# The feed-forward layer's last casts and products written ahead of the first expert's steps; rank and table transposes written later

## The chip, the cores and the metric

One core of a Trainium2 chip runs the kernel. The metric is the device time in microseconds (us) of one execution; the time before is the median of three runs. Matrix products run on TensorE (PE, with its weight loads as PEld), elementwise work on VectorE (DVE), ScalarE (ACT) and GpSimd (POOL); SyncE (SP) issues most transfers.

## What is computed

Three layers in float32: a gated linear attention (4 sequences of 768 tokens, 8 heads of 48), a feed-forward layer with softplus (384 to 2048 to 384), and a layer of 8 experts of which each token takes at most one.

```python
# attention: state = f * state + k (x) v ; y = q . state          -> x [3072, 384]
h = x @ w_in
g = np.maximum(h, 0.0) + np.log1p(np.exp(-np.abs(h)))
x = g @ w_out
# experts
do_compute = x @ w_skip > 0
logits = xc @ w_gate                      # xc = x[do_compute]
e_idx = np.argmax(logits, axis=1)
gate_w = softmax(logits)[e_idx]
y[mask] = gate_w[mask, None] * (np.maximum(xc[mask] @ w1[e], 0.0) @ w2[e])   # per expert e
out[do_compute] = xc + y                  # the other tokens keep x
```

## The kernel before

The 3072 tokens are worked in 12 units of 256. Every float32 operand of a large product is split into a high part (fp32r) and a low part, and three products of the parts stand for one. The attention runs in 24 chunks of 128 tokens and is worked in between the feed-forward layer's steps.

**The feed-forward layer.** A unit has 8 steps (`STEPS`), one for every 256 hidden columns. `Ffn.up` (L396) makes 18 products into a PSUM tile `ph`; `ph` and the experts' `phm` share two PSUM buffers (tag "h"). `act_a` (L411 to L416) computes exp(-|h|) and max(h, 0) into tiles `u` and `w`, `act_b` (L422, L423) the logarithm on ACT and the sum on POOL (on DVE for the very last step of the last unit, which is also worked in two halves, `FINE`), `act_c` (L431, L432) casts the result to `gh` and `gl`. `down` (L443) adds 12 products into `acc0` and `acc1`, one per 128 tokens. `u`, `w`, `gh` and `gl` have two buffers each. The loop over s (L853) writes step s's `up`, the step before's `act_b` and `act_c`, and the `down` of the step before that; the program text numbers the last unit's steps 0 to 7, and s = `total` - 1 is step 7. What the loop leaves over, `act_b` and `act_c` of step 7 and `down` of steps 6 and 7, is written in the part after it.

**Routing.** After a unit's last `down`, `evac` copies `acc` out on ACT, `logits` and `choose` find each token's expert on DVE, `rank` (L502, L503 on PE, then DVE) gives each token its place in that expert's list, and `scatter` (L511, POOL) writes token numbers into a table in DRAM. `table_cols` (L538) loads that table back with eight transfers on SP into a tile `rows`, which takes one of the two `u` buffers, turns it with two PE transposes (`pids`, L547) and copies it to `tab`. Unit 11's tokens do not go through the table: `last_rank` ranks them and builds one-hot tiles (`place`, L518 to L527), and `last_ids` multiplies these on PE (`placed`, L533, `pplace`) and adds `tab`; the sum is the list of token numbers that the remaining gathers need. `flag_counts` sets the flag for the general path.

**The experts.** The fullest expert is worked first, its first 256 tokens (`firsts`) from a list that is ready earlier. `turn` (L694, `pxg`, then L373 and L374) transposes the gathered rows; four steps follow, each with `Tiles.up` (L711, 18 products into `phm`), `act` (L720, L721) and, one step later, `down` (L756, 24 products into `pom`, which takes the PSUM buffers of `acc0` and `acc1`). The loop over `at` (L1018) writes these steps, with `later` as the list of `down`s still to come. `turn` of `firsts` stands at s = `total` - 3.

**Order.** The program text is not the final order. A scheduler places each engine's instructions by the order of writing and its own picture of when inputs are ready; where `pin` is on (it is switched on in `last_down`), an instruction keeps its place in the text. The engines run their rows strictly in order.

Of the kernel before, what the change touches and what calls it, by code (L numbers as in the profile page):

```python
# [37 lines left out]
def gla_softplus_moe_kernel(  # L38
# [17 lines left out]
    NCH, PR, _ = q.shape  # L56
# [14 lines left out]
    STEPS = NF // 2  # L71
# [480 lines left out]
    def set_turns():  # L552

        pc = psm("pfirst")
        te.matmul(pc[:, 0:E], lhsT=ones, rhs=cnt_acc[:, 0, :], start=True, stop=True)
        tmp = lambda nm, n: ffn.tile([P, n], F32, tag="t" + nm, name="t" + nm, bufs=1)
        c, mx, at, neg = tmp("c", E), tmp("m", 1), tmp("a", E), tmp("n", E)
        ve.tensor_tensor(c, pc[:, 0:E], ebase, op=ALU.subtract)
        ve.tensor_reduce(mx, c, axis=AX.X, op=ALU.max)
        ve.scalar_tensor_tensor(c, c, mx, down8, op0=ALU.is_ge, op1=ALU.mult)  # L560
        ve.tensor_reduce(mx, c, axis=AX.X, op=ALU.max)

        ve.tensor_scalar(at, down8, mx, -1.0, op0=ALU.subtract, op1=ALU.mult)
        ve.tensor_scalar(neg, at, 0.0, float(E), op0=ALU.is_lt, op1=ALU.mult)
        ve.tensor_tensor(at, at, neg, op=ALU.add)
        ve.tensor_scalar(erot, at, float(NT), float(-BIG), op0=ALU.mult, op1=ALU.add)
        ve.tensor_scalar(c, down8, -1.0, float(E), op0=ALU.mult, op1=ALU.add)
        ve.tensor_tensor(perm, at.unsqueeze(1).to_broadcast([P, E, E]), c.unsqueeze(2).to_broadcast([P, E, E]),
                         op=ALU.is_equal)
        ve.tensor_scalar(c, c, mx, float(E), op0=ALU.subtract, op1=ALU.add)  # L570
        ve.tensor_scalar(neg, c, float(E), float(-E), op0=ALU.is_ge, op1=ALU.mult)
        ve.tensor_tensor(turns, c, neg, op=ALU.add)
        expert_at.extend(nc.values_load(turns[0:1, e:e + 1], engines=[sy.engine], min_val=0, max_val=E - 1)
                         for e in range(E))
# [51 lines left out]
    def w_load(n):  # L626
        e, g = n // 4, n % 4
        raw[n] = w_tile(n, F32)
        src = (w1 if g < 2 else w2)[ds(expert_at[e], 1), g % 2].rearrange("o p c -> (o p) c")
        sy.dma_start(out=raw[n].rearrange("p a c -> p (a c)"), in_=src)  # L630
# [16 lines left out]
    def feed(n):  # L647

        while True:
            while wanted and len(slots) >= (1 if wanted[0][0] == "load" else 2):  # L650
                what, q = wanted.pop(0)
                if what == "load":
                    w_load(q)
                else:
                    pieces.extend(w_split(q))
            if n <= 0 or not pieces:
                return
            w_piece(*pieces.pop(0))
            n -= 1
# [140 lines left out]
    if True:  # L800
# [22 lines left out]
        def attention_step(s):  # L823
            for c, nm in sorted(todo.pop(s, []), key=lambda x: (x[0], order[x[1]])):
                ops[nm](c)
# [5 lines left out]
        def route_step(u, i):  # L831
            if u < 0 or u >= NU:
                return
            if i == 1:
                routes[u] = Route(ffns[u], u * UNIT, tid[:, u * CPU:(u + 1) * CPU], *([pools["pre"], cnt_last] if u == NU - 1 else []))
            for at, nm, *a in ROUTE if u < NU - 3 else ROUTE_SOON if u < NU - 1 else ():
                if at == i:
                    getattr(routes[u], nm)(*(a if nm != "rank" else [cnt_acc[:, 0, :]]))
            if i == 2 and 0 < u < NU - 2:
                routes[u - 1].scatter(1)  # L840
# [3 lines left out]
        def conv(s, j):  # L844
            if s in CONV_AT:
                g = CONV_AT.index(s)
                if j % 2:
                    conv_w(g, j // 2)
                if j == 3 and g + 2 < STEPS:
                    load_w(g + 2)  # L850
        total = NU * STEPS
        last_att = 4 * NCH - 2 - STEPS
        for s in range(-20, total):  # L853
            u, i = divmod(s, STEPS)
            conv(s, 0)
            if s > 0:
                pu, pi = divmod(s - 1, STEPS)
                ffns[pu].act_b(pi)
            conv(s, 1)
            if s >= 0:  # L860
                if i == 0:
                    ffns[u] = Ffn(xhl[u], FINE if u == NU - 1 else ())
                ffns[u].up(i)
            if s > 0:
                ffns[pu].act_c(pi)
            if s >= 0:
                ffns[u].act_a(i)
            conv(s, 2)
            attention_step(s + STEPS + 1)
            conv(s, 3)  # L870
            if s >= 2:
                pu, pi = divmod(s - 2, STEPS)
                ffns[pu].down(pi)
            route_step(u - 1, i)
            if s == total - 2 * STEPS:
                set_turns()
                for n in range(4):
                    w_load(n)
            if s == last_att:
                first.close()  # L880
                pools["pre"] = rest.enter_context(tc.tile_pool(name="pre", bufs=1, side="right", reuse_waits="tile"))
                slots += [("pre", f"w{i}") for i in range(5)]
                wanted += [("split", n) for n in range(4)] + [("load", n) for n in range(4, 12)] + [("split", n) for n in range(4, 8)]
                for e in range(2, E):
                    wanted += [("split", n) for n in range(4 * e, 4 * e + 4)]
                    if e + 1 < E:
                        wanted += [("load", n) for n in range(4 * e + 4, 4 * e + 8)]
            if u == NU - 1:
                slots.append(("wp", f"s{i}"))
                if pu == u and pi % 2:  # L890
                    slots.extend(("wp", f"s{STEPS + pi - 1 + n}") for n in range(2))
            if s > last_att:
                feed(PIECES if s <= last_att + 4 else 1)
            if s == last_att + 2:
                first_ids()
                firsts = Tiles(0, [id0[:, 0, t:t + 1] for t in range(2)], ("acc0", "acc1"))
                firsts.fetch([id0[:, 1, t:t + 1] for t in range(2)], NT - 2 * UNIT)
            if s == total - 4:
                table_cols()
                last_base()  # L900
            if s == total - 3:
                firsts.turn()
                flags()
# [91 lines left out]
    ffn_end = ffns[NU - 1]  # L995
# [10 lines left out]
    def last_rank():  # L1006
        last.rank(cnt_all)
        last.place()

    def last_ids():  # L1010
        set_ids(last.placed())
        flag_counts()

    later = [[(ffn_end.down, STEPS - 2)], [(last_down,)]]
    seq = [(w, i) for w in work for i in range(len(w.steps))]
    fetched, turned = 1, 1
    ffn_end.act_b(STEPS - 1)
    for at in range(len(seq) + 2):  # L1018
        if at < len(seq):
            w, i = seq[at]  # L1020
            while pieces and pieces[0][0] <= 4 * w.e + (1 if i == 0 else 3):
                w_piece(*pieces.pop(0))
            now, then = w.steps[i]
            for f, *args in now:
                f(*args)
            if at == 0:
                ffn_end.act_c(STEPS - 1)
            turn_at = 0 if w.n == 1 else 3 if w is firsts else 2
        for _ in range(2 if len(later) > 1 and (at == 2 or (at > 2 and w.n == 2 and i)) else 1):
            for f, *args in later.pop(0) if later else ():  # L1030
                f(*args)
        if at < len(seq):
            later += then
        feed(FILL[at])
        if at == 1:
            last_rank()
        elif at == 2:
            last_ids()
        if at >= 2 and at < len(seq):
            k0 = work.index(seq[at][0])  # L1040
            while fetched < len(work) and fetched <= k0 + 1:
                work[fetched].fetch(work[fetched].cols)
                fetched += 1
            if turned == k0 + 1 and turned < fetched and i == turn_at:
                work[turned].turn()
                turned += 1
# [9 lines left out]
    with tc.If(some > 0, preferred_fallthrough_block=False), ExitStack() as gen:  # L1056
# [23 lines left out]
        for e in range(E):  # L1080
            n = nc.values_load(cnt[0:1, e:e + 1], min_val=0, max_val=NT)
            with tc.If(n > 0):
# [6 lines left out]
                with tc.For_i(0, (n + (P - 1)) // P, 1) as it:  # L1089
# [3 lines left out]
                    w = Tiles(e, [c[:, 1:2]], ("acc0",))  # L1093
# [75 lines left out]
```

## Time and profile before

| | us |
|---|---|
| median of 3 runs | 752.81 (750.46 to 754.51) |
| the profiled execution | 751.03 |
| its span in the trace | 749.3 |
| outside the span | 1.73 |
| PE busy | 688.8 (92%) |
| DVE busy | 538.5 (72%) |
| ACT busy | 477.2 (64%) |
| POOL busy | 199.3 (27%) |

The sums of the prediction are made against the profiled execution, and the difference is then put on the median. PE is busy nearly all the time, so a look at the whole tells little; what counts is where PE stands still. A timeline row gives start, duration, engine, line, tiles and, in brackets, the idle time before it and what ended it. A matmul's end is modelled and lies about one matmul behind the start of the next, so from one start to the next is the better measure of lost time.

### The profile page before, as it was taken

Reading aid. Unit: us, or ns where it says so; the run is one execution under the profiler, and the core shown is the slowest. Engines: PE = TensorE matmul, PEld = TensorE weight load, DVE = VectorE, ACT = ScalarE, POOL = GpSimd, SP = SyncE. Lnnn points to the kernel's source line nnn. Section 1 sums busy time; section 2 is a strip of 40 time slices with the busy share of each in tenths; the row PEclk is TensorE's granted clock in tenths of the full one; section 3 lists DMA queues with packets and bytes.
Section 4 is the critical chain, followed back from the end, with each engine's and each line's share of the span. In section 5 each row is a group of like instructions: output and inputs, shape, how many; then the busy total and the mean of one; then the engine's idle time right before and its main releaser. Section 6 shows DMA issues by size and latency. Waiting matters only on the chain. (4 is left out here: it accounts for less than half of the span.)

```text
span 749.3 us, 15063 instructions
## 1 busy us (share of the span) xinstructions
PE 688.8 (92%) x5869; PEld 639.8 (85%) x5869; DVE 538.5 (72%) x1081; ACT 477.2 (64%) x864; POOL 199.3 (27%) x170
## 2 busy tenths in 40 slices
PE   1788889999999999999999999999979979999993
PEld 1576768989999999999999999999969878989893
DVE  6989999867777677778767777756667555866851
ACT  5596777767666766766686666656567634555750
POOL 1204212322222323222232322223333204222111
PEclk9989999999999999999999999999999999999997
DMA  9944423202132121212212121100606412555910
GB/s 278 282 159 147 151 66 111 80 26 74 55 82 73 50 64 52 87 56 76 77 41 70 45 85 44 61 9 1 210 22 219 166 43 82 189 210 198 324 43 11
DMA packets 33905, 77.19 MB, mean 103 GB/s; under 512 B 5967, under 2 KB 18594, under 8 KB 33824
## 3 DMA queue, kind: packets, MB, share of 16 engines
q1 hardware_dynamic: 31456, 71.89, 29.7%
q0 software_dynamic: 2368, 4.25, 2.0%
q8 instruction: 48, 0.79, 0.5%
q14 instruction: 33, 0.27, 0.1%
HBM read 64.89 MB, written 12.11 MB: 103 GB/s over the span
## 5 line engine op out<-in xcount | busy, mean ns | idle before, releaser
L396 PE MATMUL ph<-xh,wi 128*128 128x256 f32 x1152 | 229.1, 288 | 3.2 <-ACT wi L215 1.6
L423 POOL TENSOR_TENSOR w<-w,u 128x512 f32<-128x512 f32 x95 | 129.3, 1361 | 354.0 <-DVE u L416 204.5
L396 PEld LDWEIGHTS ph<-xh,wi 128*128 128x128 f32 x1152 | 187.2, 192 | 8.2 <-ACT wi L215 2.3
L396 PE MATMUL ph<-xl,wi 128*128 128x256 f32 x576 | 163.9, 285 | 0.0
L443 PE MATMUL acc<-wo_hi,gh 128*128 128x394 f32 x384 | 137.8, 360 | 2.2 <-ACT gh L431 2.2
L443 PE MATMUL acc<-wo_hi,gl 128*128 128x394 f32 x384 | 130.1, 346 | 3.8 <-DVE gl L432 3.6
L443 PE MATMUL acc<-wo_lo,gh 128*128 128x394 f32 x384 | 131.7, 343 | 0.0
L396 PEld LDWEIGHTS ph<-xl,wi 128*128 128x128 f32 x576 | 110.8, 192 | 0.0
L432 DVE TENSOR_TENSOR gl<-w,gh 128x512 fp32r<-128x512 f32 (+1 forms) x97 | 67.0, 692 | 43.1 <-ACT gh L431 42.5
L415 DVE SCALAR_TENSOR_TENSOR u<-w,u 128x512 f32<-128x512 f32 (+1 forms) x97 | 66.7, 689 | 34.3 <-ACT w L413 33.9
L411 ACT ACTIVATE u<-ph 128x512 f32<-128x512 f32 (+1 forms) x97 | 56.9, 587 | 46.5 <-PE ph L396 44.9
L422 ACT ACTIVATE w<-w 128x512 f32<-128x512 f32 (+1 forms) x97 | 60.9, 628 | 37.0 <-DVE u L415 36.9
L443 PEld LDWEIGHTS acc<-wo_hi,gh 128*128 128x128 f32 x384 | 72.4, 189 | 7.9 <-ACT gh L431 3.3
L431 ACT CAST gh<-w 128x512 fp32r<-128x512 f32 (+1 forms) x97 | 59.2, 611 | 30.4 <-POOL w L423 26.2
L443 PEld LDWEIGHTS acc<-wo_hi,gl 128*128 128x128 f32 x384 | 72.6, 189 | 5.4 <-DVE gl L432 5.1
L443 PEld LDWEIGHTS acc<-wo_lo,gh 128*128 128x128 f32 x384 | 73.1, 190 | 0.2 <-DVE wo_lo L243 0.2
L416 DVE SCALAR_TENSOR_TENSOR u<-ph,u 128x512 f32<-128x512 f32 (+1 forms) x97 | 65.9, 680 | 3.3
L641 DVE TENSOR_TENSOR w<-w,w 128x768 fp32r<-128x768 f32 x64 | 59.5, 973 | 7.5 <-ACT w L640 4.7
L412 ACT ACTIVATE u<-u 128x512 f32<-128x512 f32 (+1 forms) x97 | 60.7, 627 | 1.6
L413 ACT ACTIVATE w<-u 128x512 f32<-128x512 f32 (+1 forms) x97 | 60.5, 625 | 1.4
L756 PE MATMUL pom<-w,gh 128*128 128x384 f32 x208 | 54.2, 342 | 2.5 <-DVE om L766 2.5
L640 ACT CAST w<-w 128x768 fp32r<-128x768 f32 x64 | 49.8, 837 | 3.1 <-DMA w<-in_moe_w_dram 2.3
(194 smaller groups left out, 1134.6 us busy)
## 6 DMA issues: line engine op xcount, KB each, us to landing
w<-in_moe_w_dram SPq DMA_DIRECT2D x32, 768.0 KB
si<-in_moe_w_in_dram SPq DMA_DIRECT2D x8, 768.0 KB
so<-in_moe_w_out_dram SPq DMA_DIRECT2D x8, 768.0 KB
f<-in_f_logit_dram SPq DMA_DIRECT2D x24, 227.5 KB
q<-in_q_dram SPq DMA_DIRECT2D x24, 224.0 KB
k<-in_k_dram SPq DMA_DIRECT2D x24, 224.0 KB
x_s<-xr SPq DMA_DIRECT2D x24, 192.5 KB
v<-in_v_dram SPq DMA_DIRECT2D x24, 192.0 KB
```

The source lines that it names most:

```text
L396: te.matmul(ph[:, j, :], lhsT=w[i][:, kk, j * P:(j + 1) * P], rhs=x[:, kk, :], start=(n == 0), stop=(n == 3 * KD - 1))
L411: se.activation(u[:, c], ph[:, c], AF.Abs)
L412: se.activation(u[:, c], u[:, c], AF.Exp, scale=-1.0)
L413: se.activation(w[:, c], u[:, c], AF.Identity, bias=1.0)
L415: ve.scalar_tensor_tensor(u[:, c], w[:, c], 1.0, u[:, c], op0=ALU.subtract, op1=ALU.subtract)
L416: ve.scalar_tensor_tensor(u[:, c], ph[:, c], 0.0, u[:, c], op0=ALU.max, op1=ALU.subtract)
L422: se.activation(w[:, c], w[:, c], AF.Ln)
L423: (ve if i in self.fine else ge).tensor_tensor(w[:, c], w[:, c], u[:, c], op=ALU.add)
L431: se.copy(flat(gh)[:, c], w[:, c])
L432: ve.tensor_tensor(flat(gl)[:, c], w[:, c], flat(gh)[:, c].bitcast(F32), op=ALU.subtract)
L443: te.matmul(self.acc[t][:, 0:XR], lhsT=g[:, j, t * P:(t + 1) * P], rhs=w[f // 4][:, f % 4, :], start=(f == 0 and n == 0), stop=(f == NF - ...
L641: pin(ve.tensor_tensor(lo, t, hi.bitcast(F32), op=ALU.subtract))
```

## The change

`table_cols` and `last_base` move from s = `total` - 4 to s = `total` - 2, that is, behind the last `turn` and the flags. `down` of step 6 and `act_c` of step 7 move ahead of the experts' loop; `later` starts with an empty entry instead. `last_rank` moves from the end of round `at` = 1 into round `at` = 2, behind the first `down` of the experts that this round writes. Nothing is added or removed: each engine has as many instructions as before.

```diff
-            if s == total - 4:
+            if s == total - 2:
                 table_cols()
                 last_base()
             if s == total - 3:
...
-    later = [[(ffn_end.down, STEPS - 2)], [(last_down,)]]
+    later = [[], [(last_down,)]]
     seq = [(w, i) for w in work for i in range(len(w.steps))]
     fetched, turned = 1, 1
     ffn_end.act_b(STEPS - 1)
+    ffn_end.down(STEPS - 2)
+    ffn_end.act_c(STEPS - 1)
     for at in range(len(seq) + 2):
...
-            if at == 0:
-                ffn_end.act_c(STEPS - 1)
             turn_at = 0 if w.n == 1 else 3 if w is firsts else 2
-        for _ in range(2 if len(later) > 1 and (at == 2 or (at > 2 and w.n == 2 and i)) else 1):
+        for n in range(2 if len(later) > 1 and (at == 2 or (at > 2 and w.n == 2 and i)) else 1):
             for f, *args in later.pop(0) if later else ():
                 f(*args)
+            if at == 2 and n == 0:
+                last_rank()
         if at < len(seq):
             later += then
         feed(FILL[at])
-        if at == 1:
-            last_rank()
-        elif at == 2:
+        if at == 2:
             last_ids()
```

Two places show what this does to the engines' rows. The first is the end of the feed-forward layer on PE. Before, from the last product of step 4's `down` (`acc1`, `gl_7417`) to the first of the experts' `phm0`; `ph7` is step 7's `up`, `wo_hi2_119` with `gh_7486` step 5's `down`:

```order
L443 MATMUL acc1_7230<-wo_hi2_119,gl_7417 128x394
L547 MATMUL pids_7387<-ident_79,rows_7378 128x96
L694 MATMUL pxg_7445<-ident_79,xg_7124 128x128 x3
L694 MATMUL pxg_7451<-ident_79,xg_7128 128x128 x3
L784 MATMUL pm_7459<-ident_79,hm_7457 1x128
L785 MATMUL pm_7459<-ident_79,col0_98 1x128
L396 MATMUL ph7_7515<-xh11_6650,wi7_114 128x256
...
L547 MATMUL pids_7387<-ident_79,rows_7378 128x96
L443 MATMUL acc0_7229<-wo_hi2_119,gh_7486 128x394
...
L711 MATMUL phm0_7573<-xh_7443,w0_7061 128x256
```

The same place in the changed kernel (`gh_7469` is step 5's `down`, `gh_7534` and `gl_7535` step 6's):

```order
L443 MATMUL acc1_7230<-wo_hi2_119,gl_7400 128x394
L396 MATMUL ph7_7515<-xh11_6650,wi7_114 128x256
...
L711 MATMUL phm0_7591<-xh_7426,w0_7061 128x256
...
L443 MATMUL acc0_7229<-wo_hi2_119,gh_7469 128x394
...
L443 MATMUL acc0_7229<-wo_hi3_121,gh_7534 128x394
...
L547 MATMUL pids_7505<-ident_79,rows_7496 128x96
L443 MATMUL acc0_7229<-wo_hi3_121,gl_7535 128x394
```

The two table transposes now stand around the second part of step 6's `down`; `pxg` and `pm` are gone from here, since they now stand 102 products earlier, beside unit 10's rank; and `phm0` follows step 7's `up` directly. The same stretch on POOL, before, from step 2's sum (`w_7223`); `table` is the scatter of unit 10's two halves, and the last two sums are those of steps 5 and 6:

```order
L423 TENSOR_TENSOR w_7223<-w_7223,u_7222 128x512
L511 DMA table_76<-tid_87,rslot_7264 24576x1
L423 TENSOR_TENSOR w_7302<-w_7302,u_7301 128x512
L511 DMA table_76<-tid_87,rslot_7264 24576x1
L423 TENSOR_TENSOR w_7358<-w_7358,u_7357 128x512
L423 TENSOR_TENSOR w_7421<-w_7421,u_7420 128x512
L423 TENSOR_TENSOR w_7491<-w_7491,u_7490 128x512
```

And in the changed kernel:

```order
L423 TENSOR_TENSOR w_7223<-w_7223,u_7222 128x512
L423 TENSOR_TENSOR w_7302<-w_7302,u_7301 128x512
L511 DMA table_76<-tid_87,rslot_7264 24576x1
L423 TENSOR_TENSOR w_7358<-w_7358,u_7357 128x512
L511 DMA table_76<-tid_87,rslot_7264 24576x1
L423 TENSOR_TENSOR w_7404<-w_7404,u_7403 128x512
L423 TENSOR_TENSOR w_7474<-w_7474,u_7473 128x512
```

Both scatters have moved one sum later, and the second now stands ahead of step 5's sum instead of step 4's. The second place is unit 11's rank on PE, before, from the last product of step 7's `down`:

```order
L443 MATMUL acc1_7230<-wo_hi3_121,gl_7597 128x394
L502 MATMUL pr_7678<-roh_7663,before_83 128x16
L503 MATMUL pr_7678<-cnt_last_94,ones_82 128x16
L711 MATMUL phm2_7703<-xh_7443,w1_7063 128x256
...
L756 MATMUL pom_7727<-w2_7069,gl_7634 128x384
L533 MATMUL pplace_7752<-pcol_7696,prow_7695 128x192
```

And in the changed kernel, where `gl_7611` is the last product of the experts' first `down`:

```order
L443 MATMUL acc1_7230<-wo_hi3_121,gl_7586 128x394
L711 MATMUL phm2_7678<-xh_7426,w1_7063 128x256
...
L756 MATMUL pom_7702<-w2_7069,gl_7611 128x384
L502 MATMUL pr_7715<-roh_7663,before_83 128x16
L503 MATMUL pr_7715<-cnt_last_94,ones_82 128x16
L756 MATMUL pom_7701<-w2_7069,gh_7633 128x384
...
L533 MATMUL pplace_7752<-pcol_7733,prow_7732 128x192
```

The rank has moved behind 18 products of `phm2` and 12 of `pom`; between it and `pplace` stand 12 products now, where 42 stood. On DVE the change in the chain between these two is one row (the difference of the two kernels):

```order
 L506 TENSOR_TENSOR rw<-pr,roh 128x16
+L721 SCALAR_TENSOR_TENSOR gl<-phm_7678,gh 128x512
 L507 TENSOR_REDUCE rrk<-rw 128x2
 L508 TENSOR_SCALAR rslot<-rrk 128x2
...
 L526 TENSOR_SCALAR prow<-place,rcols 128x128
 L527 TENSOR_SCALAR pcol<-place,rcols,rless 128x192
-L721 SCALAR_TENSOR_TENSOR gl<-phm_7703,gh 128x512
```

The low part of `phm2`'s result now stands inside the rank's chain. SP's rows are the same.

## Rows read from the trace of the kernel before

**Rows 1.** The page, busy time and share of the span by engine.

```profile
PE 688.8 (92%) x5869; PEld 639.8 (85%) x5869; DVE 538.5 (72%) x1081; ACT 477.2 (64%) x864; POOL 199.3 (27%) x170
```

**Rows 2.** Windows: length, busy time of PE, PEld, DVE, ACT, POOL, granted clock, DMA.

```profile
592.00:613.00 21.00, 15.53 (x107) 14.28 (x106) 11.89 (x35) 10.50 (x24) 2.55 (x2) 1.00 0.07 23
700.00:720.00 20.00, 20.00 (x112) 17.99 (x111) 16.50 (x22) 15.17 (x24) 2.90 (x2) 1.00 0.62 240
```

**Rows 3.** PE's timeline, 592 to 613 us: the rows around its four stops.

```profile
592.25 0.34 PE L443 MATMUL acc<-wo_hi,gl 128*128 128x394 f32 x1
593.91 0.27 PE L547 MATMUL pids<-ident,rows 96*128 96x96 f32 x1 [1.33 <-DMA rows<-table]
...
599.12 0.34 PE L443 MATMUL acc<-wo_hi,gl 128*128 128x394 f32 x1
600.86 0.36 PE L711 MATMUL phm<-xh,w 128*128 128x256 f32 x1 [1.40 <-DVE u L416]
...
607.19 0.34 PE L443 MATMUL acc<-wo_hi,gl 128*128 128x394 f32 x1
607.84 0.45 PE L443 MATMUL acc<-wo_hi,gh 128*128 128x394 f32 x1 [0.32 <-ACT gh L431]
...
609.74 0.52 PE L443 MATMUL acc<-wo_hi,gl 128*128 128x394 f32 x2
612.68 0.36 PE L502 MATMUL pr<-roh,before 128*128 128x16 f32 x2 [2.42 <-DVE xr L489]
```

**Rows 4.** PE's timeline: first rows of two `phm` groups, of what follows each, and `pplace`.

```profile
603.79 0.28 PE L711 MATMUL phm<-xh,w 128*128 128x256 f32 x1
...
605.92 0.35 PE L443 MATMUL acc<-wo_hi,gl 128*128 128x394 f32 x1
...
613.12 0.41 PE L711 MATMUL phm<-xh,w 128*128 128x256 f32 x1
...
616.86 0.51 PE L756 MATMUL pom<-w,gh 128*128 128x384 f32 x2
...
621.07 0.81 PE L533 MATMUL pplace<-pcol,prow 128*128 128x192 f32 x4
```

**Rows 5.** Windows (columns as above): behind the longest stop, and behind a stop of 1.76 us.

```profile
612.60:617.00 4.40, 4.32 (x23) 4.35 (x24) 2.29 (x14) 0.00 (x0) 0.00 (x0) 0.61 0.34 120
675.00:680.00 5.00, 4.82 (x33) 4.82 (x34) 2.73 (x4) 1.33 (x3) 2.95 (x2) 1.00 0.55 157
```

**Rows 6.** Timelines of ACT and DVE: `act_a` of steps 5, 6 and 7.

```profile
595.82 0.61 ACT L411 ACTIVATE u<-ph 128x512 f32<-128x512 f32 x1
597.32 0.38 ACT L411 ACTIVATE u<-ph 128x256 f32<-128x256 f32 x1 [0.90 <-PE pids L547]
...
592.43 0.69 DVE L416 SCALAR_TENSOR_TENSOR u<-ph,u 128x512 f32<-128x512 f32 x1
...
600.03 1.02 DVE L416 SCALAR_TENSOR_TENSOR u<-ph,u 128x512 f32<-128x512 f32 x2
```

**Rows 7.** Timelines of PE (end of step 5's `up`), POOL (scatters, a sum) and SP (eight loads).

```profile
585.98 0.34 PE L443 MATMUL acc<-wo_hi,gh 128*128 128x394 f32 x1
...
579.42 1.22 POOL L511 DMA_INDIRECT table<-tid,rslot  x1 [0.83 <-DVE rslot L508]
...
586.12 1.02 POOL L511 DMA_INDIRECT table<-tid,rslot  x1 [3.91 <-DMA table<-tid,rslot]
587.14 1.32 POOL L423 TENSOR_TENSOR w<-w,u 128x512 f32<-128x512 f32 x1
...
590.60 3.90 SPq L542 DMA_DIRECT2D rows<-table  x8
```

**Rows 8.** DVE's timeline: first and last row of the rank's chain, and `phm2`'s low part.

```profile
613.31 0.17 DVE L506 TENSOR_TENSOR rw<-pr,roh 128x16 f32<-128x16 f32 x1 [0.37 <-PE pr L503]
...
615.09 0.38 DVE L527 TENSOR_SCALAR pcol<-place,rcols,rless 128x192 f32<-128x192 f32 x1
...
619.62 0.69 DVE L721 SCALAR_TENSOR_TENSOR gl<-phm,gh 128x512 fp32r<-128x512 f32 x1 [4.15 <-ACT gh L720]
```

## Prediction

> **What bounds the kernel now.** I read the page first: PE is busy 92% of the span, the next engine 72% [rows 1]. So what a change is worth is the time in which PE stands still or runs slowly, and only in the stretch that the change touches. The windows show where: between 592 and 613 us PE is busy 15.53 of 21 us, while later stretches such as 700 to 720 us have no idle time at all [rows 2]. PE's timeline then names the four stops of that stretch and what ended each [rows 3]: the table transposes wait for the `rows` load, the experts' first `phm` for DVE to have read step 6's `ph`, step 7's `down` for its cast, and unit 11's rank for the routing chain on DVE.
>
> I measure a stop from start to start, less one product. A product takes 0.18 us: 24 of them run from 616.86 to 621.07 [rows 4]. The stops then cost 593.91 - 592.25 - 0.18 = 1.48, 600.86 - 599.12 - 0.18 = 1.56, 607.84 - 607.19 - 0.18 = 0.47, and 612.68 - (609.74 + 0.18) - 0.18 = 2.58 us [rows 3], together 6.09.
>
> The last stop has a sequel. The 18 products of `phm` take 605.92 - 603.79 = 2.13 us before it and 616.86 - 613.12 = 3.74 us after it [rows 4]; the granted clock of that stretch is 0.61, so part of it ran at 1.2 instead of 2.4 GHz [rows 5]. That is another 1.61 us. In all 7.70 us are lost here.
>
> **The change, part by part.** The instructions stay the same on every engine, so the sum is made of waits alone.
>
> *The table's load and transposes.* The first stop goes, because step 7's `up` no longer stands behind the transposes. The load has a second effect that the stop's row does not show. `rows` holds one of the two `u` buffers from its load, issued at 590.60 [rows 7], until PE has turned it: step 6's first ACT row starts only at 595.82 and step 7's at 597.32, the latter released by `pids` [rows 6]. So DVE reads step 6's `ph` as late as 600.03 [rows 6], and this is what the experts' first `phm` waits for. With `rows` asked for after step 6's tiles, steps 5 and 6 have both buffers, and the second stop should go with the first.
>
> What is late next? I count from the end of step 5's `up` (585.98 before, [rows 7]). PE then has 12 + 18 + 12 products until step 7's `up`, 592.25 + 0.18 - 585.98 = 6.45 us [rows 3, 7]. That `up` needs the PSUM buffer that DVE frees with step 5's L416, which before ended at 592.43 + 0.69 = 593.12, or 7.14 after the same point [rows 6]. In the changed order ACT takes step 5's first row earlier but puts three weight casts into the middle of the chain. So PE waits between 0 and 0.7 us here; I take 0.5, near the row. Step 6's two DVE rows follow, 1.4 us, to 8.5; PE gets to `phm0` at 7.14 + 2.13 = 9.3, so that wait is nil with 0.8 us to spare.
>
> POOL and SP: the load may go once POOL has read step 5's `u`. Its log on ACT and its sum (1.32 us, [rows 7]) should be done by 8.5 + 1.3 = 9.8. The first transpose could start 593.91 - 590.60 = 3.31 us after the first load was issued, [rows 3, 7], so at 13.1; PE gets there at 9.3 + 2.13 + 16 x 0.18 = 14.3. The second needs the last four loads. All eight take 3.90 us to issue; the fourth was issued by 592.55 and had landed 1.36 later, so the eighth is there 3.90 + 1.36 = 5.3 after the first, at 15.1, and PE comes at 14.3 + 0.1 + 8 x 0.18 = 15.8. No wait, with 0.7 to 1.2 us to spare. The load also needs the second scatter. The scatters stand one sum later on POOL, behind a rank result that now has four DVE rows of up to 0.69 us [rows 6] more ahead of it; that makes some 3 us, so 582.5 in the clock of before. The second started 6.70 us after the first, since it waits for the first one's landing, and landed 3.46 us after its end [rows 7]; by the same steps it now lands at 582.5 + 6.7 + 1.0 + 3.5 = 593.7, against 585.98 + 9.8 = 595.8 for the sum. What stands behind the second scatter on POOL is step 5's sum instead of step 4's, and that one is not ready before it either. So I cost the scatters at nothing; the cover is 2 us.
>
> The transposes of the gathered rows and the flag move forward into a stretch where PE is full. They cost the same there as they did here, so this is nothing, from both sides.
>
> *Step 6's `down` and step 7's cast and products.* Between the two halves of step 7's `down` now stand the 18 products of `phm1`, 2.13 us, so the second half's cast has time. I let the third stop go, 0.47 us, with 0 as the other end.
>
> *The rank.* The fourth stop was 2.58 us of waiting for the copy of `acc` and the choice. Now `phm2` (2.13) and 12 products (2.1) stand ahead of the rank, 4.2 us, so the wait is covered. `pom` takes over `acc0` and `acc1`, so its first product needs the copy; that copy was the first part of the same 2.58 us, and `phm2` alone covers 2.13 of them. At most 0.5 us, taken as nothing. With the stop the slow clock should go too: behind a stop of 1.76 us at 675 us the clock stayed at 1.00, behind this one it fell to 0.61 [rows 3, 5], and no stop that I now expect is over 0.7 us.
>
> The price is a new wait at `pplace`. The rank's chain on DVE ran from 613.31 to 615.09 + 0.38, that is to 2.79 us after the rank's start at 612.68 [rows 3, 8]. Now `phm2`'s low part, 0.69 [rows 8], stands inside it: 3.48. PE has the rank itself (0.44, to 613.12) and 12 products (2.1) to do until then: 2.54. So PE waits at most 0.94 us where it had been covered by 42 products; the first of the two pairs is ready earlier, so I take 0.6, with 0 to 0.94 as bounds. All later gathers wait for this list as before, at the same distance.
>
> **The sum.** 6.09 + 1.61 - 0.5 - 0.6 = 6.6 us. Behind `pplace` the order is the same, with PE at 20.00 of 20 us from 700 to 720 [rows 2], so I carry it to the end: 751.03 - 6.6 = 744.4 for the profiled execution. The median of the three runs is 1.78 above that execution, so 752.81 - 6.6 = **746.2**.
>
> **The rivals.** *The clock term is not there.* Where PE's clock falls may depend on more than the length of the stop before it, and then an ordinary execution of before may not have paid the 1.61 us, or the changed one pays it at another stop. The row shows one fall behind 2.58 us of waiting and none behind 1.76 us [rows 5], which leaves this open. The gain is then 5.0 and the time 747.8. The Trainium skill, "TensorE: Matmul & The Clock Gate", section "What's actually happening", says that the activity window runs freely and does not start with the kernel, which speaks for this rival; the one execution traced here cannot show it.
>
> *The gain is given back later.* The last stretch also splits and loads weights, with DVE at 16.50 and ACT at 15.17 of 20 us [rows 2]. If these set the pace there, an earlier start of the experts only makes PE wait for them. PE's full window speaks against it. Half given back is 749.5, all of it 752.8.
>
> *Slower: the table's load comes late.* The transposes stand at the head of PE's row inside step 6's `down`, the load is issued some 5 us later than before, and the two scatters stand in a chain ahead of it. The cover is 1.2 us for the first transpose and 0.7 for the second; from there on every microsecond costs one. To be slower than before it has to be late by 6.6 on top, to be slower by 0.5% by over 10 us. The first scatter's landing took 586.12 - 580.64 = 5.5 us with the weight loads running [rows 7], so 10 more is far. At 11 us late the time is about 757.
>
> *It does nothing.* The order shows that the rows move, so this would need the waits to come back in full in the new places; 752.8.
>
> **How the numbers follow.** Forecast 0.62, clock rival 0.18, given back 0.13, late load 0.04, nothing 0.03. A measurement of this kernel can tell about 0.5% from no change, 3.8 us. The forecast and the clock rival lie below 749.05, so faster 0.80; given back and nothing make same 0.15, with the late load's small cases; slower 0.05. The predicted time is the forecast's. The low end is no new waits, 7.7, and a median that falls nearer to the profiled execution: 743.5. The high end takes in the clock rival and the gain half given back: 750.0.
>
> **What would show it.** In the changed kernel's trace step 7's `up` starts within 0.7 us of step 4's last product, `phm0` follows it without a stop, `pids` is released by nothing, and the rank comes after 12 products without a wait. PE waits 0.3 to 0.9 us at `pplace`, for DVE. The clock is 1.00 from 592 us to there. From step 4's last product to `pplace` it takes 21 to 22 us, where it took 621.07 - 592.25 = 28.8 [rows 3, 4]: less the 6.6, and less the transposes that moved away. A stop ended by `rows` shows the late load; the same `pplace` gain with a span that is not shorter shows the gain given back, and then the stops behind 640 us name what took it.

## The result

| | before | after |
|---|---|---|
| median of six runs, us | 752.35 (750.46 to 754.86) | 743.67 (739.19 to 744.44) |
| ratio | | 0.9877, 95% interval 0.9851 to 0.9902 |
| the profiled execution, us | 751.03 | 744.39 |
| its span | 749.3 | 742.6 |

The change is faster. The forecast for the profiled execution was 744.4, and it took 744.39. For the median the forecast was 746.2, and 743.67 was measured. By the ratio the gain is 1.23% of 752.35, or 9.3 us, which makes 743.1, where 6.6 was forecast and 7.7 was the most that the sum allowed. So the steps have to be looked at first, and then the way from one profiled execution to a median.

PE's busy time has hardly changed against [rows 1]; the span is shorter:

```profile
PE 688.3 (93%) x5869; PEld 639.4 (86%) x5869; DVE 537.4 (72%) x1081; ACT 477.2 (64%) x864; POOL 198.0 (27%) x170
```

The windows view over the same 21 us as in [rows 2] (length, busy time of PE, PEld, DVE, ACT, POOL, granted clock, DMA) has PE at 20.45 us where it had 15.53:

```profile
592.00:613.00 21.00, 20.45 (x141) 20.08 (x140) 12.33 (x37) 9.94 (x22) 2.83 (x2) 1.00 0.13 44
```

PE's timeline of the changed kernel, at the places that answer to [rows 3, 4] (start, duration, engine, line, tiles; in brackets the idle time before it and what ended it):

```profile
592.84 0.34 PE L443 MATMUL acc<-wo_hi,gl 128*128 128x394 f32 x1
593.73 0.36 PE L396 MATMUL ph<-xh,wi 128*128 128x256 f32 x1 [0.55 <-DVE u L416]
...
595.96 0.28 PE L711 MATMUL phm<-xh,w 128*128 128x256 f32 x1
...
600.99 0.25 PE L547 MATMUL pids<-ident,rows 96*128 96x96 f32 x1
...
606.92 0.28 PE L711 MATMUL phm<-xh,w 128*128 128x256 f32 x1
...
609.06 0.51 PE L756 MATMUL pom<-w,gh 128*128 128x384 f32 x2
...
611.16 0.29 PE L502 MATMUL pr<-roh,before 128*128 128x16 f32 x2
...
613.54 0.34 PE L756 MATMUL pom<-w,gl 128*128 128x384 f32 x1
613.93 1.08 PE L533 MATMUL pplace<-pcol,prow 128*128 128x192 f32 x4
```

One bracket is left, 0.55 us at step 7's `up`. `phm0`, `pids` and the rank have none. From step 4's last product to `pplace` it is 613.93 - 592.84 = 21.09 us, where it was 28.82. Part of that difference is the transposes of the gathered rows and the flag, which have moved ahead of this place. Counted from unit 10's rank, which stands ahead of their old and of their new place, it is 37.23 us where it was 44.17, so 6.9 less. The view of line 533 shows the new wait at `pplace`, in two pieces, one ahead of each pair of products:

```profile
its engine sat idle before it (us, times) until:
  DVE pcol L527: 0.6, 2
```

Of these 0.6 us, 613.93 - 613.54 - 0.18 = 0.2 lie ahead of the first product of `pplace` and about 0.4 behind it.

### The profile page after: what moved, and what is told of

Its sections match the earlier page's. It is cut to its first block, busy times and chain, and to the rows that moved or that the text cites. A ratio compares the mean times of both kernels' runs of the same rounds, so it can differ in the third digit from the quotient of the medians.

```text
span 742.6 us, 15067 instructions
## 1 busy us (share of the span) xinstructions
PE 688.3 (93%) x5869; PEld 639.4 (86%) x5869; DVE 537.4 (72%) x1081; ACT 477.2 (64%) x864; POOL 198.0 (27%) x170
```

## The experiments

The theory was the prediction's: the gain is the stops on PE with the slow clock behind the longest of them, and what was measured beyond that is the draw: executions of one kernel differ, and quick ones of the changed kernel happened to be timed. The first rival was that the clock falls by chance and not with the stop. The second was that the change saves time at another place too.

**Both kernels again.**

> The kernel before once more, for a second trace and for the clock of each of its executions. The theory (four stops of 6.09 us on PE, and 1.61 us of slow clock behind the longest of them): the ratio to itself is 1.000 within 0.003; the second trace has the same four stops, 1.4 to 1.6, 1.5 to 1.6, 0.4 to 0.6 and 2.5 to 2.7 us, and the 18 products behind the last take about 3.7 us again, at a granted clock near 0.6. The rival (where the clock falls is chance): the four stops are the same, but the 18 products take 2.1 to 3.0 us, and the low clock lies elsewhere. A third theory (the profiled execution of before happened to be quick): its span is 750.5 to 753 us this time, and what is longer lies outside 592 to 617 us.

> The changed kernel once more. All theories: ratio 0.985 to 0.992, step 4's last product to pplace in 20.8 to 21.6 us. The theory (the gain is 6.6 us, and what was measured beyond that is how the low clock fell in the executions that were timed): the executions differ by their clock, those at 0.989 are 3 to 5 us shorter than those at 0.977 to 0.982, and the trace shows the low stretches outside the changed place. The rival (the change also saves time in a later or earlier stage): at an equal mean clock the changed kernel is still 8 us or more shorter than the kernel before.

Measured: the kernel before against itself 0.9995 (0.9967 to 1.0023); the changed kernel 0.989 (0.9854 to 0.9927). In the comparison of the changed kernel, one execution had a mean clock of 0.989 and took 741.85, four less than the one at 0.980, as the theory has it. Those with a mean clock of 0.980 to 0.986 took 745.5 in the mean of five, and 751.2 in the mean of 19 of the kernel before. That is 5.7 us at about the same clock, not the 8 or more of the second rival (such a comparison leaves out the slow clock that the change itself removes). In the second trace of before, whose span is 749.8, the first stop is 595.73 - 594.41 - 0.18 = 1.14 us, less than the 1.4 to 1.6 expected; the others are as they were. The rank's stop is the same to the hundredth, but the clock did not fall. PE's timeline and a window from the rank's start:

```profile
614.52 0.37 PE L502 MATMUL pr<-roh,before 128*128 128x16 f32 x2 [2.42 <-DVE xr L489]
...
614.96 0.36 PE L711 MATMUL phm<-xh,w 128*128 128x256 f32 x1
...
617.18 0.51 PE L756 MATMUL pom<-w,gh 128*128 128x384 f32 x2
```

```profile
614.40:618.90 4.50, 4.38 (x32) 4.41 (x33) 2.33 (x14) 0.00 (x0) 0.00 (x0) 1.00 0.34 119
```

The 18 products took 617.18 - 614.96 = 2.22 us, not 3.74 as in [rows 4]. So the clock term is not in every execution, and it had to be counted.

**One part alone: the table.**

```diff
-            if s == total - 4:
+            if s == total - 2:
                 table_cols()
```

> One part alone: the table's load, its transposes and what goes with them are written later; the casts, step 6's down and the rank stand as before. The theory by the stops: the first two stops go (1.48 + 1.56 us) and step 7's up waits about 0.5 us for DVE, so 2.5 us are gained, ratio 0.9967; the rank's stop of 2.5 us and the 18 slow products behind it stay. The rival (part of the gain of both is in this part, by a later or earlier stage): 4 us or more, ratio 0.9945 or less, with the rank's stop still in the trace.

Measured: 0.9939 (0.9908 to 0.9971). PE's timeline has step 7's `up` with the 0.56 us, transposes that wait for nothing, and the rank's stop:

```profile
595.72 0.36 PE L396 MATMUL ph<-xh,wi 128*128 128x256 f32 x1 [0.56 <-DVE u L416]
...
602.98 0.25 PE L547 MATMUL pids<-ident,rows 96*128 96x96 f32 x1
...
611.43 0.40 PE L502 MATMUL pr<-roh,before 128*128 128x16 f32 x2 [2.32 <-DVE roh L492]
```

The third stop, ahead of the second half of step 7's `down`, is gone as well, which the expectation did not have. From unit 10's rank to `pplace` it takes 41.19 us, against 44.27 in the mean of the four traces of before with a fall of like length (below): 3.1 us. That is the two stops and the third, less the 0.7 us at `up`: 1.48 + 1.56 + 0.47 - 0.7 = 2.8, and 0.1 of the rest is the rank's stop, which is 0.1 shorter here. The 4.6 us of the ratio lie on the rival's side (4 or more), but with bounds of 2.2 to 6.9 they don't decide; that the rank's stop and its slow clock are still there, and that it is 128.03 us from `pplace` to the end as before (table below), speaks against a gain at another stage.

**One part alone: the rank.**

```diff
             for f, *args in later.pop(0) if later else ():
                 f(*args)
+            if at == 2 and n == 0:
+                last_rank()
...
-        if at == 1:
-            last_rank()
-        elif at == 2:
+        if at == 2:
             last_ids()
```

> One part alone: the rank of unit 11 is written behind the first down of the experts; the table and the casts stand as before. The theory by the stops and the clock: 2.58 + 1.61 us go and 0.6 us of waiting at pplace come, so 3.6 us are gained, ratio 0.9952, and the 18 products of phm2 take 2.1 to 2.2 us. The rival (the clock falls anyway): 2.0 us, ratio 0.9973, and the low clock lies at another place behind 592 us. The other rival (the rest of the gain sits here): 5.5 us or more, ratio 0.9927 or less.

Measured: 0.9953 (0.9928 to 0.9977), which is 3.5 us, as the theory has it. The trace has `pids` waiting 1.55 us and `phm0` 1.40 us as before, the rank without a stop, and `phm2` in 2.13 us. From step 4's last product to `pplace`, less the wait at `pids`, it takes 25.10 - 1.55 = 23.55 us; the second trace of before, which has no fall either, takes 26.98 - 0.98 = 26.00. That is 2.45 us, the stop of 2.58 less the 0.2 ahead of `pplace`.

**The rank undone in the changed kernel** (the difference above, backwards).

> The changed kernel with the rank of unit 11 put back to where it stood before; table and casts as changed. All theories: the stop of 2.3 to 2.4 us ahead of the rank is back, the first three stops stay away, and the wait at pplace is gone. The theory that the clock falls behind such a stop in some executions only: the 18 products of phm2 take 3.6 us or 2.2 us in this trace, either way, and the time on average is that of the table alone less about 0.2, ratio 0.994 within 0.002; from unit 10's rank to pplace 40.9 us with the fall or 39.4 without. The theory of the prediction (it always falls): 3.6 us, 40.9, ratio 0.9955 within 0.002.

Measured: 0.9946 (0.9922 to 0.9969). The stop is back, 2.32 us, the 18 products took 3.63 us, and step 4's last product to `pplace` is 24.97 us against 21.09 in the changed kernel. So the rank's part is worth 3.9 us up to `pplace` in an execution in which the clock falls. It had fallen in this one; by the time, the two theories are not told apart.

**One part alone: the casts.**

```diff
-    later = [[(ffn_end.down, STEPS - 2)], [(last_down,)]]
+    later = [[], [(last_down,)]]
...
     ffn_end.act_b(STEPS - 1)
+    ffn_end.down(STEPS - 2)
+    ffn_end.act_c(STEPS - 1)
...
-            if at == 0:
-                ffn_end.act_c(STEPS - 1)
```

> The part that is left, alone: step 6's down and step 7's cast are written ahead of the experts' loop, table and rank stand as before. All theories: the first two stops and the rank's stop stay as they were (1.0 to 1.6, 1.4, 2.4 us idle). The prediction's step: the stop of 0.47 us ahead of the second half of step 7's down goes, ratio 0.9994, not to be told from 1 by the time. The rival (this part does nothing by itself, since in the table's part alone that stop had gone without it): the stop stays. The rival that seeks the missing gain here: 0.9975 or less.

Measured: 0.9993 (0.9968 to 1.0018). In PE's timeline the third stop is gone and the others are there. So the part does what it says (26.67 - 1.24 = 25.43 us from step 4's last product to `pplace` less the wait at `pids`, against 26.00), but the table's part takes the same stop away, and the two do not add. In this trace too, 2.42 us of waiting were followed by a clock of 1.00:

```profile
592.23 0.27 PE L547 MATMUL pids<-ident,rows 96*128 96x96 f32 x1 [1.24 <-DMA rows<-table]
...
599.18 0.36 PE L711 MATMUL phm<-xh,w 128*128 128x256 f32 x1 [1.41 <-DVE u L416]
...
610.44 0.37 PE L502 MATMUL pr<-roh,before 128*128 128x16 f32 x2 [2.42 <-DVE xr L489]
```

**How often the clock falls behind the rank's stop.** Four more traces of the kernel before, unchanged.

> The kernel before, one trace more, to count how often the clock is low behind the rank's stop. In four traces with that stop so far it was low three times, in six without it never. The theory (the stop makes the fall likely, not certain): in four more traces it is low in two to three, and then the 18 products of phm2 take 3.6 to 3.8 us, else 2.2. The rival (the fall depends on how long the low stretch at 555 us lasted): it is low exactly where that stretch lasted 3.4 us, and not where it lasted 6.8.

> As the run before it, a second trace. The theory: two to three falls in four; the stop itself is 2.4 us each time. The rival: low exactly where the stretch at 555 us was short.

> As above, a third trace. The same numbers; and from unit 10's rank to pplace 44.2 us with the fall, 42.7 without.

> As above, a fourth trace. The same numbers; and from unit 10's rank to pplace 44.2 us with the fall, 42.7 without.

Measured, with the traces so far ("clock" is the granted clock of the 4.5 us from the rank's start; 1.00 is 2.4 GHz, 0.50 is 1.2 GHz):

| trace | idle ahead of the rank | clock | 18 products of `phm2` | step 4's last product to `pplace` | of it idle at `pids` | unit 10's rank to `pplace` | `pplace` to the end |
|---|---|---|---|---|---|---|---|
| before, as profiled at first | 2.42 | 0.61 | 3.74 | 28.82 | 1.33 | 44.17 | 128.23 |
| before, second | 2.42 | 1.00 | 2.22 | 26.98 | 0.98 | 42.75 | 128.41 |
| c1_before | 2.42 | 0.50 | 3.98 | 29.90 | 1.05 | 46.38 | 129.79 |
| c2_before | 2.42 | 0.62 | 3.60 | 28.90 | 1.38 | 44.36 | 128.06 |
| c3_before | 2.42 | 0.65 | 3.34 | 28.85 | 1.35 | 44.23 | 129.46 |
| c4_before | 2.42 | 0.64 | 3.36 | 28.65 | 1.15 | 44.31 | 128.10 |
| table alone | 2.32 | 0.62 | 3.59 | 25.05 | none | 41.19 | 128.03 |
| rank undone | 2.32 | 0.62 | 3.63 | 24.97 | none | 41.11 | 128.14 |
| casts alone | 2.42 | 1.00 | 2.23 | 26.67 | 1.24 | 42.09 | 128.18 |
| after, six traces | none | 1.00 | 2.13 to 2.14 | 21.08 to 21.12 | none | 37.23 in each | 128.32 to 130.33 |
| rank alone | none | 1.00 | 2.13 | 25.10 | 1.55 | 40.75 | 129.73 |

It fell in all four of the new traces, where two to three had been expected, and the 18 products took 3.34 to 3.98 us, a wider spread than the 3.6 to 3.8 expected. With the stop that makes seven of nine traces, and five of six of the kernel before. Without it, it never fell here. Step 4's last product to `pplace` less the wait at `pids` is 26.00 us without a fall, 27.5 in four traces and 28.85 in c1_before: a fall costs 1.5 us, once 2.85. The widest case, c1_before, as PE's timeline and windows have it; in the first 4.5 us all is at 0.50, and it is low still behind them:

```profile
611.68 0.58 PE L502 MATMUL pr<-roh,before 128*128 128x16 f32 x2 [2.42 <-DVE xr L489]
...
612.53 0.56 PE L711 MATMUL phm<-xh,w 128*128 128x256 f32 x1
...
616.51 0.84 PE L756 MATMUL pom<-w,gh 128*128 128x384 f32 x2
```

```profile
611.60:616.10 4.50, 4.42 (x21) 4.45 (x22) 2.29 (x14) 0.00 (x0) 0.00 (x0) 0.50 0.33 117
611.50:619.00 7.50, 7.32 (x33) 7.35 (x34) 2.38 (x15) 0.00 (x0) 0.00 (x0) 0.57 0.21 75
```

The rival that ties the fall to the low stretch at 555 us is out: c2_before, c3_before and c4_before had the longer stretch there (granted clock 0.77 to 0.80 from 550 to 565 us, against 0.89 in the first trace) and fell behind the rank's stop all the same.

**Is the rest of the gain real?** With these traces the theory's sum can be made as a mean. From unit 10's rank to `pplace` the kernel before takes 44.37 us in the mean of its six traces, the changed one 37.23 in each of six: 7.1 us. Behind `pplace`, in traces with a clock of 1.00 at the stop near 672 us, it is 128.16 us in the mean of the seven traces of kernels with the rank's stop and 128.57 in four of the changed kernel: 0.4 us given back, the second half of the wait at `pplace`. That leaves 6.7 us, where the ratios of the first two comparisons give 9.3 and 8.3. A gain at another place isn't in the traces: ahead of unit 10's rank and from `pplace` on, the rows of every engine stand in the same order in both kernels. The time from the start to unit 10's rank was even 1.4 us longer in the mean of the changed kernel's six traces (578.2 against 576.8); it runs from 575.0 to 579.8 in the kernel before alone, so that is draw. Four more series:

> The changed kernel a third time, beside the others of this call, for more executions and one more trace. All theories: from unit 10's rank to pplace 37.2 us within 0.1. The theory (6 to 7 us are gained, the first comparison drew quick executions): ratio 0.990 to 0.992. The rival (more than 8 us are gained on average): 0.987 to 0.9895.

> The changed kernel, for more executions beside those of the kernel before. The theory (6.7 us, which is what the traces account for on average: 7.1 up to pplace less 0.4 behind it): the ratio of all runs together comes down to 0.990 to 0.992. The rival (8 us, of which 1.4 lie outside the place that the change touches): it stays at 0.988 to 0.9895.

> As the run before it. The theory: 0.990 to 0.992; the rival: 0.988 to 0.9895. In the trace: from step 4's last product to pplace 21.1 us, granted clock 1.00 there.

> As the two before it. The theory: 0.990 to 0.992; the rival: 0.988 to 0.9895. In the trace: from step 4's last product to pplace 21.1 us, granted clock 1.00 there.

Measured: 0.9896 (0.9863 to 0.9928), 0.9936 (0.9908 to 0.9965), 0.9895 (0.9863 to 0.9927) and 0.9915 (0.9885 to 0.9944). Taken by itself the first stands between the theory's and the rival's values, the second misses both, the third is the rival's and the fourth the theory's; with their bounds none of them decides. In each trace it is 21.1 us from step 4's last product to `pplace`. All executions together, 92 of the kernel before and 45 of the changed one, have medians of 751.63 and 744.77 and means of 752.00 and 744.93. The difference of the means is 7.1 us, 6.2 to 7.9 (95%, by resampling the executions), and the ratio of the means 0.9906. So the theory's 6.7 is inside, and the 8 us of the rival are just outside.

**Another stop of the same kind.** In both kernels PE stands still for 2.1 to 3.0 us near 555 us, since DVE's `gl` waits behind six splits of the experts' weights. The changed kernel's timeline:

```profile
554.18 0.45 PE L443 MATMUL acc<-wo_hi,gh 128*128 128x394 f32 x1 [1.23 <-ACT gh L431]
...
558.17 0.70 PE L443 MATMUL acc<-wo_hi,gl 128*128 128x394 f32 x1 [2.99 <-DVE gl L432]
```

DVE's timeline there, with the six splits and `gl`:

```profile
550.33 6.58 DVE L641 TENSOR_TENSOR w<-w,w 128x768 fp32r<-128x768 f32 x6
...
557.43 0.68 DVE L432 TENSOR_TENSOR gl<-w,gh 128x512 fp32r<-128x512 f32 x1
```

Two kernels tried to take it away, by splitting less at first (the second has `feed(1)` in that place):

```diff
-                feed(PIECES if s <= last_att + 4 else 1)
+                feed(1 if s <= last_att + 4 else PIECES)
```

> The changed kernel with one more edit, at another place: behind the attention the experts' weights are split one piece a step for four steps and two a step after that, where it was two and then one. The stop of 3.0 us at 555 us (PE waits for DVE's gl, which stands behind six splits of 1.1 us) should shrink, since only four stand there and gl comes ahead of the next step's u. The theory (a stop costs itself and, in some executions, a slow clock behind it): the stop falls to under 0.8 us, and the low clock of 3.4 to 6.8 us of time behind it (granted clock 0.77 to 0.89 from 550 to 565 us in all six traces) goes as well; 3.8 to 5.5 us less than the changed kernel, ratio to the kernel before 0.983 to 0.986. The rival (the clock falls somewhere anyway): 2.2 us less, 0.988. The other rival (the splits that come later cost the experts' first steps their cover): the stop shrinks but the time does not, 0.991, with new stops between 590 and 640 us.

> As the run before, but one piece a step throughout, so that more splits are left for the experts' loop. The theory: the same stop goes, and if the late splits have cover there, the time is that of the run before within 1 us. The rival: PE waits for the splits or for the loads that their buffers let go, 2 us or more behind 615 us.

Measured: 0.9955 (0.9934 to 0.9977) and 0.9904 (0.988 to 0.9928); the first is slower than the changed kernel, the second the same. The long stop goes, but another grows beside it, from 1.23 to 1.9 us, and the clock still falls there, if for less time (0.89 from 550 to 565 us in both, 0.77 to 0.84 in the six traces of the changed kernel). Then new stops come at 584 to 597 us. In the first of the two:

```profile
553.54 0.44 PE L443 MATMUL acc<-wo_hi,gh 128*128 128x394 f32 x1 [1.90 <-ACT gh L431]
...
584.12 0.45 PE L443 MATMUL acc<-wo_hi,gh 128*128 128x394 f32 x1 [1.44 <-ACT gh L431]
...
594.83 0.44 PE L443 MATMUL acc<-wo_hi,gh 128*128 128x394 f32 x1 [1.06 <-ACT gh L431]
...
597.07 0.45 PE L443 MATMUL acc<-wo_hi,gl 128*128 128x394 f32 x1 [1.24 <-DVE gl L432]
```

Both edits moved the scheduler's order of DVE, ACT and PE from 552 to about 605 us, and not only the splits. What the theory said of the low clock and of the time was wrong, and of the stop it was right only for the one that waits for `gl`. The rival with new stops behind 590 us was right in kind for the first kernel, but two of its four stops lie elsewhere, and at 0.9955 it is slower than the 0.991 of that rival. For the second kernel neither expectation held: it took 744.68, 4.2 us less than the first, where 1 us was allowed, and has no stop behind 615 us that the changed kernel lacks.

## Why the prediction was right, and where it missed

*The first two stops: right.* `pids` waits for nothing and `phm0` follows step 7's `up`. The new wait at that `up` was taken as 0.5 and is 593.73 - 592.84 - 0.18 = 0.71, at its bound of 0.7. The rival of a late table load is out: no stop ended by `rows` stands in any trace of the changed kernel.

*The third stop: right in size, not in its cause.* The cast has time, but it has that with the table's part alone too, and with the casts alone.

*The rank: right.* It comes after 12 products without a wait. `pplace` waits 0.6 us, as taken.

*The clock term: near the mean in size, by the luck of the one trace, and for a reason that did not hold.* By the table its cost in the six traces of before is none once, 1.5 us four times and 2.85 us once, 1.48 in the mean, where 1.61 was taken from one trace. The argument for it, that behind 1.76 us the clock stays at 1.00 [rows 5], is wrong: behind that very stop it fell in seven of 18 traces. The timeline of c3_before, and the window around it:

```profile
673.34 0.85 PE L756 MATMUL pom<-w,gh 128*128 128x384 f32 x2 [1.76 <-DVE om L766]
```

```profile
672.00:680.00 8.00, 6.66 (x35) 6.66 (x36) 3.82 (x5) 2.77 (x6) 2.95 (x2) 0.79 0.59 191
```

The rival without the clock term named the right mechanism (where the clock falls depends on more than the length of the stop) and gave it the wrong price: it took the whole term away, though it comes in five of six executions and so still moves the median. The page of the Trainium skill that was cited there ("TensorE: Matmul & The Clock Gate", section "What's actually happening") says that the activity window runs freely. That agrees with the same stop of 2.42 us being followed by 0.50, 0.61 to 0.65 and 1.00 in six traces of one kernel.

*The sum: right.* 6.6 us were forecast. The two profiled executions differ by 751.03 - 744.39 = 6.64, the traces by 6.7 in the mean, and all executions by 7.1 (6.2 to 7.9). That the profiled execution came out at 744.39 for 744.4 is luck to that degree: the six profiled executions of each kernel lie from 749.74 to 753.92 and from 744.39 to 749.61, 5.3 us apart in the mean, since the stretch ahead of unit 10's rank happened to be longer in the second six.

*From the execution to the median: this step failed.* The prediction took the 1.78 us by which the median of three runs lay above the profiled execution as an offset of the kernel, and put it on the changed one as well. It was the draw of three runs: the median of 92 executions is 751.63, 0.60 above that execution. 751.63 - 6.6 = 745.0, and the median of 45 executions of the changed kernel is 744.77. Of the 2.5 us between 746.2 and 743.67, 1.2 are the offset (1.78 for 0.60), 1.1 the draw of the first six executions of the changed kernel and 0.2 the sum. The ratio's 9.3 us has the draw of both sides: in the first comparison the kernel before stood 0.7 us above its long-run median, and the changed one 1.1 below its own; both errors push the same way.

*The range: too narrow below.* Its low end, 743.5, was the largest sum of the mechanism, 7.7, and a smaller offset, with no room for the draw; 743.67 lies just above it, and the 743.1 of the ratio below. But executions of one kernel lie apart by more than the whole gain: 745.7 to 757.3 before, 739.2 to 750.3 after. Their standard deviation is 2.2 us before and 2.4 after, so that even the mean of six is good to no more than 0.9 to 1.0 us. The two quickest of the first six of the changed kernel had a mean clock of 0.989 and spans of 740.3 and 737.5; those at 0.977 and 0.982 had 741.5 to 742.7.

*What stays open.* Whether the 0.4 us between the 6.7 of the traces and the 7.1 of all executions is anything: the interval of the latter is 0.8 to each side.

## What to carry to other kernels

A gain worked out stop by stop from PE's timeline can be right within half a microsecond over the place that is changed and still miss the median by 2 to 3 us, so take the spread of the executions that are shown into the range, and do not add an offset that rests on three runs. Price the slow clock behind a stop as a chance times a cost, from several traces if there are any, since one trace says neither that it falls nor that it doesn't. And before a stop is taken away by moving work in a scheduled program, look at what else the scheduler moves: the splits' burst went, and its cost came back as four shorter stops.

## What the runs showed of the hardware

That behind one and the same wait of PE the granted clock falls in some executions and not in others, and behind 1.76 us too, where the first trace had shown no fall: near 555 us, where a wait of 2.1 to 3.0 us stands a few us behind others of up to 1.8 us, in 16 of 16 traces (granted clock of 550 to 565 us 0.77 to 0.89), behind 2.3 to 2.4 us ahead of the rank in seven of nine, behind 1.76 us near 672 us in seven of 18. Where no wait was longer than 0.7 us, between 592 us and `pplace` in the changed kernel, it stayed at 1.00 in six of six. Nor did it fall, in any of the eight traces that have them, behind the waits of 1.0 to 1.6 us at `pids` and of 1.4 us at `phm0`. A fall cost 1.5 us ahead of `pplace`, once 2.85, and 1.1 to 1.8 us near 672 us (from `pplace` to the end, 129.46 and 129.79 against a mean of 128.16 in kernels with the rank's stop, 129.70 and 130.33 against 128.57 in the changed one).
